# Column norms of two weight matrices in an attention and MLP kernel: sums of squares over four blocks on VectorE ahead of four products, in place of sixteen products

## The chip, the core and the metric

The kernel runs on one core of one Trainium2 chip. The metric is the device time of one execution in microseconds (us). The engines are TensorE (PE, matrix products), VectorE (DVE), ScalarE (ACT), GpSimd (POOL) and SyncE (SP, which issues the DMAs here). A tile is 128 partitions by some number of elements. PE writes to PSUM, which DVE and ACT can read; POOL works on SBUF alone.

## The reference, cut to what matters

```python
a = softmax over the sequence of phi                 # per batch b, head h: 576 x 32
k_m, v_m = a^T k, a^T v                              # 32 x 64 each
attn = softmax(q k_m^T / 8) ; out = attn v_m         # 576 x 64
x = out, heads side by side                          # 4608 tokens x 512
h = x @ w_in                                         # 512 x 2048
g = h - tanh(h)
return g @ w_out                                     # 2048 x 512
```

Batch and heads are 8 and 8. The weights w_in and w_out come in float64. The column norms, which the change is about, are no part of the result. The kernel computes them to check that its fast path may be used.

## The kernel before, in words

The fast path (`split_path`) multiplies in f16 pieces: each weight is split in a high and a low f16 half, scaled by 2^13 (`win_hi`, `win_lo`, `wout_hi`, `wout_lo`), and so are the activations. It replaces tanh by a polynomial that holds for small arguments only. So the kernel gathers statistics into the tile `stat`: squared row norms of the attention values, squared column norms of both weight matrices, and a test on each weight block's exponents. `check` compares them with windows (`V_WIN`, `WI_WIN`, `WO_WIN`), `check_all` sums the outcome over the partitions with a product into `pgood`, and a general path (`wide_path`) runs after the fast one if any value lies outside. With the reference's inputs it does not run.

**Tiling.** The 4608 tokens are 18 units of 256, and the 2048 hidden columns are four blocks of 512. One turn of the main loop, called a slot here, handles one (unit, block); slot 4u + fb is unit u, block fb, so slots run from 18 to 71. In a slot PE forms the hidden tile `hs` (`mm1`, L572). ACT squares it into `u` (L579). DVE multiplies (`g1`, L587), ACT squares again (L592), DVE finishes the polynomial (`g2`, L597), and ACT copies the high half `g` (`g2_high`, L603), from which POOL makes the low half (`g3`, L608). In the next slot DVE makes four combinations of g, called forms (`a_forms`, L621, f16). In the slot after that PE multiplies with w_out (`mm2_blocks`, L708 and L715, into the PSUM tiles `x` and `o`). Where a unit is complete, DVE adds up and scales its output (`evict`, L768 to L780). `hs` is one PSUM tile, free again once g1 has read it.

**Order.** Every engine runs its instructions in the order in which the program writes them (`in_order`). The order inside a slot is: mm1, u, g1, the words of the plan's first group (`do(0)`), the second square, the forms of the slot before, g2, mm2, sums for the weight test, `do(1)`, g2_high, g3, words put off to the slot's end (`due`), evict, `do(2)`. The plan (`PLAN_C`, L861) lists words by slot; a part after `;` belongs to `do(1)`, a part after `|` to `do(2)`. Attention work of later batches is laid into the same slots by `PLAN`.

**The column norms.** `SI` (`squares_in`, L447) has ACT square one quarter of w_in, 128 x 4 x 512, into an f16 tile; `SO` (`squares_out`, L470) does the same for w_out. Both are put off to the end of their slot. `NI` (`norms_in`, L461) and `NO` (`norms_out`, L479) sum over the partitions on PE: for each group of 128 columns a product of the squares, as the stationary operand, with a column of ones gives 128 x 1. ACT then copies the 128 x 4 result out of PSUM (L466 into `stat`, L483 into `wn`). For the quarters 0 to 2 of w_in, `SS` (`squares_sum`, L452 and L453) has DVE add up the four blocks first, in two f16 adds, and four products do. For quarter 3 and for all of w_out the products sum over the blocks, so there are sixteen.

**The PSUM buffer pa.** The results of these products lie in the pool `ps_a`, whose tag "pa" has one buffer. The same buffer takes the attention's scores (`S`, L272), its products with w_in (`P`, `att_p`, L524, read by ACT at L537 and by DVE at L542), and `pgood`. PE's first product into it waits until the last reader of the tile before is done. In slots 58, 60 and 62 a `P` product follows the norm products of the slot before.

Other words of the plan in these slots: `AM` and `AD` (POOL, L302 and L315), `AT` (DVE transpose), `AS` (ACT L513, POOL L515), and `CW` (`window`, POOL's L439 on a reloaded weight block, then ACT's L443).

Of the kernel before, what the change touches and what calls it, by code (L numbers as in the profile page):

```python
# [18 lines left out]
P = 128  # L19
# [20 lines left out]
CW = (  # L40
    0.33333331252017, -0.13333128520786, 0.053934788850892, -0.021660115374759,
    0.0082189218977914, -0.0025104593252184, 0.000420695493864,
)
# [2 lines left out]

V_WIN = (2.0 ** -12, 0.0025)
WI_WIN = (1.002 * 2.0 ** -6, 1.497)
WO_WIN = (2.0 ** -6, 3.5)
N_F1 = 32  # L50
N_ROWS = 2

# [285 lines left out]
def split_path(ctx, tc, c, ins, out):  # L338
    nc = tc.nc
# [115 lines left out]
    def norms_in(fb):  # L455
        sq = acc.pop(("q", fb))
        pa = ps_a.tile([P, 2, 512], F32, tag="pa", name=f"pni{fb}")
        blocks = 1 if fb < 3 else 4
        for k in range(4):
            for pr in range(blocks):  # L460
                nc.tensor.matmul(  # L461
                    pa[:, 0, k : k + 1], sq[:, pr, P * k : P * k + P], c["ones16"],
                    start=(pr == 0), stop=(pr == blocks - 1),
                )
        o = N_F1 + 2 * B + 4 * fb
        nc.scalar.activation(stat[:, o : o + 4], pa[:, 0, 0:4], AF.Copy, scale=(S_W * S_Q) ** -2)  # L466

# [4 lines left out]
    def norms_out(part):  # L472
        if part == 0:
            acc["n"] = big.tile([P, 4, 4], F32, tag="wn", name="wn", bufs=1)
        sq = acc.pop(("q", part))
        pa = ps_a.tile([P, 2, 512], F32, tag="pa", name=f"pno{part}")
        for k in range(4):
            for i in range(4):
                nc.tensor.matmul(  # L479
                    pa[:, 0, k : k + 1], sq[:, i, P * k : P * k + P], c["ones16"],  # L480
                    start=(i == 0), stop=(i == 3),
                )
        nc.scalar.activation(acc["n"][:, :, part], pa[:, 0, 0:4], AF.Copy, scale=(S_W * S_Q) ** -2)  # L483
        if part == 3:
            o = N_CHECK - 4
            nc.vector.tensor_reduce(stat[:, o : o + 4], acc["n"], axis=AX.X, op=ALU.add)
# [311 lines left out]
    def cubic(u, fb, stay):  # L798
# [22 lines left out]
        "Z": warm, "P": att_p, "PL": att_pl, "H": mm1, "a": lambda u, fb: cubic(u, fb, False), "ap": lambda u, fb: cubic(u, fb, True), "c": lambda u, fb: g3(u, fb, nc.gpsimd), "cv": lambda u, fb: g3(u, fb, nc.vector), "PLp": att_pl_pe,  # L821
        "T": lambda x, y: conv(10 * x + y), "L": lambda x, y: low_pool(10 * x + y), "Lv": lambda x, y: low(10 * x + y), "Lp": lambda x, y: low_pe(10 * x + y),
        "G": b_form, "F": a_forms, "SI": squares_in, "NI": norms_in, "SO": squares_out, "NO": norms_out, "SS": squares_sum,
        "GG": lambda: check(tc, c, big), "GX": lambda: check_all(tc, c, ps_a),
        "M": lambda u, fb: mm2(u, fb, fb in (0, 2), fb in (1, 3)), "R": load_part, "OP": save_part, "O": save,
# [15 lines left out]
    for word in START.split():  # L841
        if ":" in word:
            k, tag = word.split(":")
# [17 lines left out]
    PLAN_C = (  # L861
# [5 lines left out]
    )  # L867
    tasks = {}
# [79 lines left out]
def check(tc, c, big):  # L948
# [4 lines left out]
    o = N_F1  # L953
    for n, (lo, hi) in ((2 * B, V_WIN), (DF // P, WI_WIN), (DM // P, WO_WIN)):
        s, g = stat[:, o : o + n], good[:, o : o + n]
# [133 lines left out]
@with_exitstack  # L1089
def tile_kernel(ctx: ExitStack, tc: tile.TileContext, qt, kva, kvt, pha, phx, w_in, w_out, out):  # L1090
    nc = tc.nc
    ins = dict(qt=qt, kva=kva, kvt=kvt, pha=pha, phx=phx, w_in=w_in, w_out=w_out)
    const = ctx.enter_context(tc.tile_pool(name="const", bufs=1))
    c = {"first": len(nc.cur_bb.bb.instructions)}
    for name, shape, dt in (
        ("ident", [P, P], F32), ("ones", [P, P], F32), ("ones16", [P, 1], F16), ("one", [P, 1], F32),
        ("beta", [P, 1], F32), ("idw", [P, P], F32), ("nidp", [P, P], F16), ("idw", [P, P], F32), ("nid16", [P, P], F16), ("stat", [P, N_CHECK], F32), ("bad", [P, 1], I32),
    ):
        c[name] = const.tile(shape, dt, name=name)
    make_identity(nc, c["ident"])  # L1100
    nc.vector.tensor_scalar(c["nid16"], c["ident"], -1.0, None, op0=ALU.mult)
    nc.vector.tensor_scalar(c["nidp"], c["ident"], -S_V * S_W / S_P, None, op0=ALU.mult)
    nc.vector.tensor_scalar(c["idw"], c["ident"], S_W, None, op0=ALU.mult)
    nc.gpsimd.memset(c["ones"], 1.0)
    nc.gpsimd.memset(c["ones16"], 1.0)
    nc.gpsimd.memset(c["one"], 1.0)
    nc.gpsimd.memset(c["beta"], BETA)
    with ExitStack() as inner:
        split_path(inner, tc, c, ins, out)
    with tc.If(c["wide"] > 0):  # L1110
        with ExitStack() as inner:
            wide_path(inner, tc, c, ins, out)
# [39 lines left out]
```

## Time and profile before

| | us |
|---|---|
| median of three runs | 660.52 (659.53 to 663.91) |
| the profiled execution | 660.23 |
| its span, first to last instruction | 658.4 |
| PE busy in the span | 640.8 (97%) |
| DVE busy | 521.8 (79%) |
| ACT busy | 373.9 (57%) |
| POOL busy | 257.0 (39%) |

The clock granted to PE was 1.0 of full speed throughout. A row of the timeline has the start and the duration in us, the engine, the line, the operation, the output and inputs with their shapes, and, where the engine stood idle before, how long and what ended it. Rows of a group joined with xN give the whole stretch. Consecutive instructions of one engine overlap a little in the rows, so what an instruction costs its engine is read from its start to the next start. In the waits, a row has the total in us, how often, and the longest.

### The profile page before, as it was taken

How to read it: one execution, taken by the hardware profiler on the slowest of the kernel's cores; microseconds unless marked ns; L12 is line 12 of the kernel's file. 1: busy time of each engine (PE TensorE's matmuls, PEld its weight loads, DVE VectorE, ACT ScalarE, POOL GpSimd, SP SyncE). 2: the span in 40 equal slices, each digit the busy share in tenths (PEclk: the TensorE clock that was granted, in tenths of full speed). 3: DMA queues.
4: the chain of work that ended last, by engine and by line, in shares of the span. 5: the costliest groups of instructions: out<-in, count | busy, mean ns of one | idle time of the engine just before them, and what ended most of it. 6: DMA issues, size and time to landing. Idle time of an engine off the chain costs nothing.

```text
span 658.4 us, 15598 instructions
## 1 busy us (share of the span) xinstructions
PE 640.8 (97%) x6690; PEld 455.9 (69%) x6690; DVE 521.8 (79%) x790; ACT 373.9 (57%) x507; POOL 257.0 (39%) x173
## 2 busy tenths in 40 slices
PE   8788999999999999999999999999999999999996
PEld 4364656655557777777776777777687777887785
DVE  6799999999855787875988679777977686867763
ACT  4577576655524456545655465545654577666541
POOL 0224331443112245442535253625452455455521
PEclk9999999999999999999999999999999999999999
DMA  8999344223223402323331524142505333234201
GB/s 340 405 366 382 107 155 140 104 88 118 76 81 102 145 20 74 113 100 135 105 113 66 168 67 152 56 147 66 157 33 195 102 104 121 65 110 139 76 33 37
DMA packets 25996, 84.98 MB, mean 129 GB/s; under 512 B 2880, under 2 KB 2880, under 8 KB 25152
## 3 DMA queue, kind: packets, MB, share of 16 engines
q1 hardware_dynamic: 24624, 81.55, 35.8%
q10 hardware_dynamic: 1296, 2.36, 0.9%
q8 instruction: 54, 0.88, 0.6%
q14 instruction: 22, 0.18, 0.1%
HBM read 72.37 MB, written 11.53 MB: 127 GB/s over the span
## 4 chain that ended last, share of the span: by engine, by line
PE 71%; DVE 15%; DMA 6%; issue 3%; POOL 2%; ACT 2%; SPq 0%; DVEq 0%; ACTq 0%; POOLq 0%
PE hs L572 20%; PE x L715 13%; PE o L708 13%; PE o L715 10%; PE o L651 5%; DMA raw<-in_w_out_dram 3%; PE pp L524 3%; PE h L572 2%; DVE wt L384 2%; DVE h L597 2%; DVE h L587 2%; PE pkv L220 2%; DMA kv<-in_kva_dram 2%; PE o1h L651 2%; DVE wt L389 1%
## 5 line engine op out<-in xcount | busy, mean ns | idle before, releaser
L608 POOL TENSOR_TENSOR g<-h,g 128x1024 f16<-128x1024 f32 x67 | 146.6, 2188 | 328.4 <-ACT g L603 215.9
L572 PEld LDWEIGHTS <-ph 128*128 128x128 f16 x2304 | 176.9, 98 | 21.1 <-issue 6.0
L572 PE MATMUL hs<-ah,ph 128*128 128x256 f16 (+3 forms) x1152 | 151.5, 246 | 0.0
L587 DVE SCALAR_TENSOR_TENSOR h<-hs,u 128x1024 f32<-128x1024 f32 x54 | 65.8, 1218 | 91.9 <-ACT u L579 91.9
L603 ACT ACTIVATE g<-h 128x1024 f16<-128x1024 f32 x72 | 76.0, 1056 | 97.5 <-DVE h L597 92.7
L572 PE MATMUL hs<-al,ph 128*128 128x256 f16 (+3 forms) x576 | 127.7, 246 | 0.0
L592 ACT ACTIVATE u<-u,beta 128x1024 f32<-128x1024 f32 x72 | 82.5, 1148 | 57.5 <-DVE h L587 57.1
L708 PE MATMUL o<-wout_hi,g 128*128 128x512 f16 x432 | 104.7, 380 | 0.0
L715 PEld LDWEIGHTS <-f 128*128 128x128 f16 x896 | 87.7, 98 | 10.1
L597 DVE SCALAR_TENSOR_TENSOR h<-u,h 128x1024 f32<-128x1024 f32 x72 | 87.6, 1217 | 0.7 <-ACT u L592 0.7
L579 ACT ACTIVATE u<-hs 128x1024 f32<-128x1024 f32 x54 | 55.0, 1019 | 54.7 <-PE hs L572 50.5
L715 PEld LDWEIGHTS <-g 128*128 128x128 f16 x672 | 64.2, 98 | 26.5 <-issue 5.1
L715 PE MATMUL x<-bt,f 128*128 128x256 f16 x672 | 82.5, 273 | 0.0
L708 PEld LDWEIGHTS <-g 128*128 128x128 f16 x432 | 40.5, 98 | 43.9 <-issue 8.1
L651 PEld LDWEIGHTS <-g 128*128 128x128 f16 x384 | 36.6, 98 | 46.7 <-issue 4.3
L621 DVE TENSOR_TENSOR f<-g 128x512 f16<-128x512 f16 x112 | 65.1, 621 | 4.3 <-POOL g L608 3.4
L651 PE MATMUL o<-wout_hi,g 128*128 128x512 f16 x192 | 59.0, 380 | 0.0
L572 PE MATMUL h<-ah,ph 128*128 128x256 f16 (+3 forms) x384 | 49.9, 246 | 0.6 <-DVE h L587 0.6
L572 PE MATMUL h<-al,ph 128*128 128x256 f16 (+2 forms) x192 | 42.5, 246 | 0.1
L542 DVE SCALAR_TENSOR_TENSOR ph<-pp,ph 128x1024 f16<-128x1024 f32 x31 | 37.7, 1215 | 0.4 <-ACT ph L537 0.3
L537 ACT ACTIVATE ph<-pp 128x1024 f16<-128x1024 f32 x32 | 32.5, 1017 | 7.7 <-PE pp L524 7.7
L651 PE MATMUL o<-wout_lo,g 128*128 128x512 f16 x96 | 36.4, 380 | 0.0
(146 smaller groups left out, 973.8 us busy)
## 6 DMA issues: line engine op xcount, KB each, us to landing
kv<-in_kva_dram SPq DMA_DIRECT2D x20, 516.0 KB, 3.9
q<-in_qt_dram SPq DMA_DIRECT2D x16, 576.0 KB, 4.3
chk<-in_w_in_dram SPq DMA_DIRECT2D x16, 512.0 KB, 5.6
chk<-in_w_out_dram SPq DMA_DIRECT2D x16, 512.0 KB, 3.3
out_dram<-r SPq DMA_DIRECT2D x27, 256.0 KB, 2.3
kv<-in_kva_dram SPq DMA_DIRECT2D x6, 1032.0 KB, 9.1
raws<-in_w_in_dram SPq DMA_DIRECT2D x12, 512.0 KB, 8.1
raw<-in_w_out_dram SPq DMA_DIRECT2D x12, 512.0 KB, 8.6
```

Of the source, the lines that this page charges most:

```text
L542: nc.vector.scalar_tensor_tensor(pl, pa, S_P / (S_V * S_W), ph, op0=ALU.mult, op1=ALU.subtract)
L572: nc.tensor.matmul(hp[:, k, tu : tu + w], px[:, g, cs], d[ax][:, g, ta : ta + w], start=(n == 0), stop=(n == 5),)
L579: nc.scalar.activation(uu, hp, AF.Square, scale=1.0 / (S_A * S_P))
L587: nc.vector.scalar_tensor_tensor(h3, hp, C2 * S_G / (S_A * S_P), uu, op0=ALU.mult, op1=ALU.mult)
L592: nc.scalar.activation(uu, uu, AF.Square, bias=c["beta"])
L597: nc.vector.scalar_tensor_tensor(h3, uu, CC, hp, op0=ALU.add, op1=ALU.mult)
L603: nc.scalar.activation(gg[:, 0], h3, AF.Copy)
L608: eng.tensor_tensor(gg[:, 1], h3, gg[:, 0], op=ALU.subtract)
L621: nc.vector.tensor_tensor(o, x, y, op=op)
L651: nc.tensor.matmul(o, gx[:, k, P * tt : P * tt + P], wx[:, 4 * fb + k, :], start=(first and k == 0 and wx is wout_hi and gx is gh), stop=( ...
L708: nc.tensor.matmul(o[th], gg[:, 0, k, P * th : P * th + P], wout_hi[:, 4 * fb + k, :], start=(first and k == 0), stop=False)
L715: nc.tensor.matmul(dst, a(1 - n, kk), b(n, kk), start=(new and kk == 0 and n == 0), stop=(end and kk == 1 and n == 1))
```

## The change

For quarter 3 of w_in and for the four quarters of w_out, DVE now adds the four blocks of squares together (the same `squares_sum`), and PE does four products instead of sixteen. The new words are SS3 in slot 55 and SS0 to SS3 in slots 57, 59, 61 and 63, all in `do(0)`, behind g1 and what `PLAN` has there. The upper and lower bound for w_out's norms become a little tighter.

```diff
-WO_WIN = (2.0 ** -6, 3.5)
+WO_WIN = (1.002 * 2.0 ** -6, 3.493)
...
     def norms_in(fb):
         sq = acc.pop(("q", fb))
         pa = ps_a.tile([P, 2, 512], F32, tag="pa", name=f"pni{fb}")
-        blocks = 1 if fb < 3 else 4
         for k in range(4):
-            for pr in range(blocks):
-                nc.tensor.matmul(
-                    pa[:, 0, k : k + 1], sq[:, pr, P * k : P * k + P], c["ones16"],
-                    start=(pr == 0), stop=(pr == blocks - 1),
-                )
+            nc.tensor.matmul(pa[:, 0, k : k + 1], sq[:, 0, P * k : P * k + P], c["ones16"], start=True, stop=True)
...
         for k in range(4):
-            for i in range(4):
-                nc.tensor.matmul(
-                    pa[:, 0, k : k + 1], sq[:, i, P * k : P * k + P], c["ones16"],
-                    start=(i == 0), stop=(i == 3),
-                )
+            nc.tensor.matmul(pa[:, 0, k : k + 1], sq[:, 0, P * k : P * k + P], c["ones16"], start=True, stop=True)
...
-        (54, "CQ CQ SI3"), (55, "CW CW CQ CQ | NI3"), (56, "CW CW CQ CQ SO0"), (57, "CW CW CQ CQ | NO0"), (58, "CW CQ SO1"),
+        (54, "CQ CQ SI3"), (55, "SS3 CW CW CQ CQ | NI3"), (56, "CW CW CQ CQ SO0"), (57, "SS0 CW CW CQ CQ | NO0"), (58, "CW CQ SO1"),
...
-        (59, "CW CQ | NO1"), (60, "CW CQ SO2"), (61, "CW CQ | NO2"), (62, "CW CQ SO3"), (63, "CW CW CQ CQ | NO3"), (64, "CW CW CQ CQ"),
+        (59, "SS1 CW CQ | NO1"), (60, "CW CQ SO2"), (61, "SS2 CW CQ | NO2"), (62, "CW CQ SO3"), (63, "SS3 CW CW CQ CQ | NO3"), (64, "CW CW CQ CQ"),
```

The order on DVE in slot 57 (unit 14, block 1), before: g1 (h3141 from hs), the four forms f140, g2, and the first instruction of the eviction. Line numbers of the changed kernel are lower by two to nine.

```order
L587 SCALAR_TENSOR_TENSOR h3141_7067<-hs_2447,u141_7065 128x1024 [waits Activation_49]
L621 TENSOR_TENSOR f140_7070<-g140_7023 128x2x256 [waits Pool_49]
L621 TENSOR_TENSOR f140_7070<-g140_7023 128x2x256
L621 TENSOR_TENSOR f140_7070<-f140_7070,g140_7023 128x2x256 [waits DVE_49]
L621 TENSOR_TENSOR f140_7070<-g140_7023,f140_7070 128x2x256 [waits DVE_49]
L597 SCALAR_TENSOR_TENSOR h3141_7067<-u141_7065,h3141_7067 128x1024 [waits Activation_49]
L768 SCALAR_TENSOR_TENSOR r130_7076<-x_2446,r130_7076 128x256 [waits DMAHW2_49,PE_49,Activation_49]
```

The same place now:

```order
L578 SCALAR_TENSOR_TENSOR h3141_7057<-hs_2447,u141_7055 128x1024 [waits Activation_49]
L452 TENSOR_TENSOR sqo0_7024<-sqo0_7024 128x1024
L453 TENSOR_TENSOR sqo0_7024<-sqo0_7024 128x512 [waits DVE_49]
L612 TENSOR_TENSOR f140_7062<-g140_7013 128x2x256 [waits Pool_49]
L612 TENSOR_TENSOR f140_7062<-g140_7013 128x2x256
L612 TENSOR_TENSOR f140_7062<-f140_7062,g140_7013 128x2x256 [waits DVE_49]
L612 TENSOR_TENSOR f140_7062<-g140_7013,f140_7062 128x2x256 [waits DVE_49]
L588 SCALAR_TENSOR_TENSOR h3141_7057<-u141_7055,h3141_7057 128x1024 [waits Activation_49]
L759 SCALAR_TENSOR_TENSOR r130_7068<-x_2446,r130_7068 128x256 [waits DMAHW2_49,PE_49,Activation_49]
```

The two adds on the squares sqo0 stand between g1 and the forms; the forms, g2 and the eviction follow behind them in the order they had.

The order on PE from the end of slot 59 (last product of mm2 into o1400, norm products pno1 on the squares sqo1, first product of the next mm1) to the first product of `P` for batch 7, block 2 (pp72) in slot 60, before:

```order
L715 MATMUL o1400_7219<-wout_lo_100,f141_7213 128x256
L479 LDWEIGHTS sqo1_7268 [waits Activation_49]
L479 MATMUL pno1_7384<-ones16_60,sqo1_7268 128x1 [waits DVE_49]
...
L572 MATMUL hs_2447<-ah6_6264,ph60_6173 128x192
...
L524 MATMUL pp72_7454<-win_hi_97,vh7_6793 32x512 [waits Activation_49]
```

The same place now:

```order
L706 MATMUL o1400_7199<-wout_lo_100,f141_7193 128x256
L473 LDWEIGHTS sqo1_7248 [waits DVE_49,Activation_49]
L473 MATMUL pno1_7366<-ones16_60,sqo1_7248 128x1 [waits PE_49]
...
L563 MATMUL hs_2447<-ah6_6264,ph60_6173 128x192
...
L515 MATMUL pp72_7424<-win_hi_97,vh7_6793 32x512 [waits Activation_49]
```

Four pairs of weight load and product are left of sixteen, and the first weight load waits for DVE's adds besides ACT's squares. The first product into pp72 waits for ACT as before, which is the copy of pno1 out of "pa". The orders on ACT, POOL and SP are as they were.

## The prediction

> **What bounds the kernel now.** I read the page first, then the waits between engines, then the timeline around the five slots that the change touches (a slot is one turn of the loop over unit and block; numbers as in PLAN_C).
>
> ```profile
> span 658.4 us, 15598 instructions
> PE 640.8 (97%) x6690; PEld 455.9 (69%) x6690; DVE 521.8 (79%) x790; ACT 373.9 (57%) x507; POOL 257.0 (39%) x173
> ```
>
> By shares PE is the bound and VectorE (DVE) has a fifth of the span free. The waits from 530 to 600 us seem to say the same:
>
> ```profile
> DVE h L587 <- ACT u L579: 17.5, 7, 3.1
> ACT u L579 <- PE hs L572: 2.3, 5, 0.7
> ```
>
> DVE idles 17.5 us there. But ScalarE (ACT), on which it waits, waited for PE only 2.3 us in 70. So there are two things that run at one pace: PE, and a ring of the other engines. One turn of the ring is ACT's square u (L579), DVE's g1 (L587), its four forms (L621) and g2 (L597), ACT's copy g (L603), GpSimd's (POOL's) subtraction (L608), and ACT's next u. DVE's idle time in it is time in which ACT does its part of the same turn; it is slack only where ACT in turn waits for PE. The change takes work from PE and puts work into the ring, between g1 and g2.
>
> **What PE saves.** The groups of four products (L461 in slot 33) and of sixteen (slot 55), each with the instruction behind it:
>
> ```profile
> 320.47 0.24 PE L461 MATMUL pni<-ones,sqi 128*128 128x1 f16 x4
> 320.58 0.27 PE L715 MATMUL x<-wout_hi,g 128*128 128x256 f16 x1
> ...
> 517.53 0.54 PE L461 MATMUL pni<-ones,sqi 128*128 128x1 f16 x16
> 517.93 0.27 PE L572 MATMUL hs<-ah,ph 128*128 128x256 f16 x1
> ```
>
> From start to start four take 0.11 us and sixteen 0.40. A group saves 0.29, five groups 1.45.
>
> The Trainium skill (TensorE: Matmul & The Clock Gate, section Back-to-back issue gap) gives about 81 ns for a pair of weight load and matmul at 128 columns. By that the sixty pairs would be 4.9 us; the trace has 25 ns a pair (0.40 / 16), since these products stream one column, and the measurement decides.
>
> **What a pair of adds costs.** The pair is not new; quarter 0 of W_in has it:
>
> ```profile
> 318.20 0.69 DVE L452 TENSOR_TENSOR sqi<-sqi 128x1024 f16<-128x1024 f16 x1
> 318.92 0.43 DVE L453 TENSOR_TENSOR sqi<-sqi 128x512 f16<-128x512 f16 x1
> 319.26 0.75 DVE L311 TENSOR_REDUCE sz<-sc 128x18 f32<-128x576 f32 x1
> ```
>
> From 318.20 to 319.26 is 1.06 us of DVE. Five pairs are 5.3. There is a second price: f16 adds of this kind can be held while POOL runs. The forms show it:
>
> ```profile
> 531.65 1.34 POOL L315 TENSOR_TENSOR sc<-sc,sz 128x576 f32<-128x576 f32 x1
> 531.90 1.37 DVE L621 TENSOR_TENSOR f<-g 128x512 f16<-128x512 f16 x1
> ```
>
> Two free forms take 0.72 us (slot 56, below); this single one took 1.37 and ended at 533.27, 0.28 after POOL's instruction (531.65 + 1.34 = 532.99). The bounds for a pair are therefore 1.06 us, and 1.06 plus one POOL instruction (1.34 here). In slots 57, 61 and 63 a form is held already, and the pair, which now stands ahead of it, is held in its place; so I take 1.06 everywhere.
>
> **Where it goes, slot by slot.** Shifts are against the profiled execution. *Slot 55*: SS3 moves g2, ACT's copy and POOL's row by 1.06; in slot 56 that meets the forms.
>
> ```profile
> 522.44 1.16 POOL L302 TENSOR_TENSOR sc<-sc,sm 128x576 f32<-128x576 f32 x1
> 523.70 0.72 DVE L621 TENSOR_TENSOR f<-g 128x512 f16<-128x512 f16 x2
> 525.13 1.22 DVE L597 SCALAR_TENSOR_TENSOR h<-u,h 128x1024 f32<-128x1024 f32 x1
> 526.39 1.06 ACT L603 ACTIVATE g<-h 128x1024 f16<-128x1024 f32 x1
> 527.35 1.89 ACT L470 ACTIVATE sqo<-wout_hi 128x2048 f16<-128x2048 f16 x1
> 529.15 1.00 ACT L579 ACTIVATE u<-hs 128x1024 f32<-128x1024 f32 x1
> ```
>
> L302 ended at 523.60, just ahead of the forms. Now it ends at about 524.7, a form waits for it, and g2 starts 0.8 late although PE brought the slot 0.29 early. ACT's three rows have no idle time between them, so u of slot 57 is 0.8 late too: the first saving of PE is lost.
>
> *Slots 57 and 58*: SS0 adds its 1.06, so g2 starts 1.8 late.
>
> ```profile
> 533.99 1.22 DVE L597 SCALAR_TENSOR_TENSOR h<-u,h 128x1024 f32<-128x1024 f32 x1
> 536.20 0.16 ACT L483 ACTIVATE wn<-pno 128x4 f32<-128x4 f32 x1
> 536.58 1.28 DVE L780 SCALAR_TENSOR_TENSOR r<-o,r 128x512 f32<-128x512 f32 x2
> 536.60 0.41 PE L524 MATMUL pp<-win_hi,vh 64*32 64x512 f16 x8
> 536.77 1.02 ACT L579 ACTIVATE u<-hs 128x1024 f32<-128x1024 f32 x1 [0.41 <-PE hs L572]
> 537.83 1.23 DVE L587 SCALAR_TENSOR_TENSOR h<-hs,u 128x1024 f32<-128x1024 f32 x1
> ```
>
> Three things hang on g2 here. Behind the copy g on ACT stands L483, which reads the column norms out of the one PSUM buffer "pa"; it ended at 536.36. PE's product L524 of slot 58 writes that same buffer and started at 536.60, 0.24 later. With L483 1.8 late PE stands at L524 until about 538.2 and everything behind it on PE waits: the saved time becomes a stall. It may wait first at the norm products themselves, for SS0's second add; L524 then still sets the time. On DVE the evictions (to L780) and then g1 follow with no idle time: g1 of slot 58 is 1.8 late. The 0.41 that u waited for PE gives nothing back, because g1 stood behind the evictions.
>
> *Slots 59 and 60*: the same pair of neighbours on "pa", now 1.8 + 1.06 = 2.9 late.
>
> ```profile
> 552.38 1.06 ACT L603 ACTIVATE g<-h 128x1024 f16<-128x1024 f32 x1 [2.15 <-DVE h L597]
> 553.35 0.16 ACT L483 ACTIVATE wn<-pno 128x4 f32<-128x4 f32 x1
> 553.62 0.41 PE L524 MATMUL pp<-win_hi,vh 64*32 64x512 f16 x8
> 553.79 1.02 ACT L579 ACTIVATE u<-hs 128x1024 f32<-128x1024 f32 x1 [0.29 <-PE hs L572]
> ```
>
> L483 ended 0.11 us before L524; PE starts it about 2.9 late. The ring could regain 0.29 at u, but a POOL row as late as g2 holds the forms of slot 60, so g2 there is 2.9 late again.
>
> *Slots 61 to 63*: SS2 makes it 4.0 on the ring, and g1 of slot 62 again stands directly behind the evictions:
>
> ```profile
> 569.37 0.16 ACT L483 ACTIVATE wn<-pno 128x4 f32<-128x4 f32 x1
> 569.83 0.41 PE L524 MATMUL pp<-win_hi,vh 64*32 64x512 f16 x8
> 571.05 1.23 DVE L587 SCALAR_TENSOR_TENSOR h<-hs,u 128x1024 f32<-128x1024 f32 x1
> ```
>
> L483 of slot 61 had 0.30 us to spare, so PE starts that L524 3.7 late. *Slot 63*: the last pair makes it 5.0. No product follows on "pa" in slot 64, so PE, 3.7 late, runs on; the ring does not catch up with it:
>
> ```profile
> 585.51 2.13 POOL L608 TENSOR_TENSOR g<-h,g 128x1024 f16<-128x1024 f32 x1 [3.77 <-issue]
> 588.34 1.76 DVE L621 TENSOR_TENSOR f<-g 128x512 f16<-128x512 f16 x2
> 590.81 1.22 DVE L597 SCALAR_TENSOR_TENSOR h<-u,h 128x1024 f32<-128x1024 f32 x1
> ```
>
> The forms of slot 64 read POOL's result and stand behind its next rows (1.76 us for two), and POOL is 5.0 late; so is g2. In slot 65 the same holds, and from slot 66 ACT's u waits for nothing. The ring meets PE at the product of the final check:
>
> ```profile
> 600.95 1.02 ACT L579 ACTIVATE u<-hs 128x1024 f32<-128x1024 f32 x1
> ...
> 623.52 0.38 PE L967 MATMUL pgood<-grow,ones 128*128 128x1 f32 x2 [0.44 <-DVE grow L960]
> ```
>
> PE waited 0.44 for the ring there, so it takes the whole lateness there at the latest: 5.0. **Sum**: 0.8 + 4 x 1.06 = 5.0 us; the 1.45 that PE saves counts only inside the 0.8. The profiled execution took 660.2 (span 658.4 and 1.8 around it), which gives 665.2; the median of the runs is 0.3 above that execution, so I say 665.3. The window constant changes two immediates of instructions that stay, which costs nothing, and no DMA is added or moved past another. If POOL did not hold the forms of slots 56, 60 and 64, the ring would regain part of that (second rival).
>
> **Rivals.** *PE's saving counts and DVE hides the adds.* For it: 97% and DVE's 17.5 us of idle time. Against it: the 0.24, 0.11 and 0.30 us on "pa", and that ACT waited for PE only 2.3 us. Time 660.2 - 1.45 = 658.8. *The ring regains its slack.* It waited for PE five times, 2.3 us, in these slots; if all is taken back, 5.0 - 2.3 = 2.7 and 662.9. It needs forms that pass POOL unheld and evictions that do not stand ahead of g1. *Clearly slower: adds and POOL hold each other.* If a pair begins inside a POOL instruction where no form was held before, each of the four pairs from slot 57 on pays one more, 1.16 us by L302's row. That makes 5.0 + 4.6 = 9.6, 669.8. It decides once the pairs, not the forms, stand at POOL's end; against it, the forms of slots 57, 61 and 63 already stand there. The Trainium skill (GPSIMD Engine Reference, section Specifications) has the two engines contend whenever DVE reads two SBUF tensors, as all ten adds do; the held form agrees. *The products are dear.* A weight load of these products lasts 96 ns by itself:
>
> ```profile
> L461 PEld LDWEIGHTS <-sqi x28: 95/96/98, 320.4 to 517.9; 128*128 128x128 f16 x28
> ```
>
> If each cost PE that much, sixty would be 5.8 us, and with PE as the bound the time 654.4. Against it: sixteen took 0.40, so the loads overlap. This is the rival in which the Trainium skill's figure for pairs, cited above, would also land, at 660.2 - 4.9 = 655.3.
>
> *It does not do what it says*: if sums in f16 left a norm outside its window, the wide path would run and add hundreds of us (it repeats PE's 640.8 us of work in f32). Weights of variance 1/512 and 1/2048 give norms near 1, far inside 2^-6 to 3.49.
>
> **How the numbers follow.** Forecast 0.59, with its own range 663.7 to 666.9 (pairs of 0.8 to 1.4 us); PE's saving 0.07; slack regained 0.22; adds and POOL 0.10; dear products 0.01; wide path 0.01. The range 661.0 to 667.8 leaves out PE's saving and most of the third rival. A measurement of this kernel can tell about 1%, 6.6 us: the forecast is +0.7%. Slower by more than that: most of the third rival, the wide path and the forecast's upper tail, 0.13. Faster: 0.01. The rest, 0.86, is within 1%.
>
> **What would show it.** Right: ten new DVE rows L452 and L453 of some 0.7 and 0.4 us, held rows among them in slot 57; PE waiting about 1 us or more for L483's successor at the product into pp in slots 58, 60 and 62; ACT's u of slots 57, 59, 61 and 63 later by about 0.8, 1.8, 2.9 and 4.0; the wait of pgood for grow above 0.44. Wrong: PE with no waits in those slots and a span below 658, or u of slot 65 less than 3 us late.

## The result, and the profile after

The changed kernel takes 665.82 us (median of seven runs, 664.93 to 668.18), the kernel before 660.90 in the same comparison (659.53 to 663.91). The ratio is 1.0064, with a 95% interval of 1.004 to 1.0087: 0.6% slower, 4.9 us. The interval leaves out 1, and the fastest of the seven changed runs lies above the slowest of the seven before. The prediction was 665.3.

The page of the changed kernel, to be read against the first two rows of the prediction:

```profile
span 664.0 us, 15493 instructions
PE 640.2 (96%) x6630; PEld 454.6 (68%) x6630; DVE 529.2 (80%) x800; ACT 374.0 (56%) x507; POOL 257.4 (39%) x173
```

PE has its sixty products less and DVE its ten adds more. Line numbers here are those of the changed kernel (g1 is L578, g2 L588, the copy g L594, u L570, the norms' copy L474, the product into pp L515). Slots 57 and 58 in its timeline, one engine after the other:

```profile
533.00 0.93 DVE L452 TENSOR_TENSOR sqo<-sqo 128x1024 f16<-128x1024 f16 x1
533.95 1.26 DVE L453 TENSOR_TENSOR sqo<-sqo 128x512 f16<-128x512 f16 x1
535.14 0.75 DVE L612 TENSOR_TENSOR f<-g 128x512 f16<-128x512 f16 x2
...
536.60 1.22 DVE L588 SCALAR_TENSOR_TENSOR h<-u,h 128x1024 f32<-128x1024 f32 x1
...
540.39 1.22 DVE L578 SCALAR_TENSOR_TENSOR h<-hs,u 128x1024 f32<-128x1024 f32 x1
...
533.33 1.60 POOL L315 TENSOR_TENSOR sc<-sc,sz 128x576 f32<-128x576 f32 x1
...
538.81 0.16 ACT L474 ACTIVATE wn<-pno 128x4 f32<-128x4 f32 x1
538.87 1.02 ACT L570 ACTIVATE u<-hs 128x1024 f32<-128x1024 f32 x1
...
535.36 0.24 PE L473 MATMUL pno<-ones,sqo 128*128 128x1 f16 x4 [1.05 <-DVE sqo L453]
...
539.02 0.41 PE L515 MATMUL pp<-win_hi,vh 64*32 64x512 f16 x8 [0.79 <-ACT wn L474]
```

The pair stands between g1 and the forms and is held by POOL's L315 in the forms' place. The two forms of this row took 1.95 us in the kernel before and take 0.75 now; before, the row was

```profile
531.33 1.95 DVE L621 TENSOR_TENSOR f<-g 128x512 f16<-128x512 f16 x2
```

PE waits first for the second add (1.05) and then for ACT's copy of the norms (0.79). g1 of slot 58 follows the evictions with no idle time.

All waits of PE from 430 us on, in the kernel before and then in the changed kernel (total, times, longest):

```profile
PE psc L272 <- DVE vl L498: 0.7, 1, 0.7
PE pgood L967 <- DVE grow L960: 0.4, 1, 0.4
PE pkv L220 <- DMA kv<-in_kva_dram: 0.3, 1, 0.3
```

```profile
PE pp L515 <- ACT wn L474: 2.2, 3, 0.8
PE pno L473 <- DVE sqo L453: 1.6, 2, 1.1
PE x L706 <- DVE r L760: 1.2, 1, 1.2
PE psc L272 <- DVE vl L489: 0.7, 1, 0.7
PE pkv L220 <- DMA kv<-in_kva_dram: 0.5, 1, 0.5
PE pgood L958 <- DVE grow L951: 0.4, 1, 0.4
PE pno L473 <- ACT r L744: 0.2, 1, 0.2
```

The first three rows and the last are new; they come to 5.2 us. PE ends up 4.75 us later (below) although it saves 1.45, so 6.2 us are to be found. The rest lies in how the rows count: a product counts as busy to the end of its row, mostly 0.27 us, while in a stream the next one starts after 0.11, so each of the seven new waits is some 0.15 us longer than its figure. The other way round, the profile shows no wait of ACT's u for PE from 531 to 601 us now, where the kernel before had 2.3 us from 530 to 600: in these slots the ring is the later of the two.

**One measure for all runs.** The first loads differ between executions by a few us (u of slot 54 starts at 502.48 before and at 503.43 in the changed kernel, and as late as 506.50 in one run below), and this moves all that follows. So I measure from ACT's u of slot 54, ahead of everything that the change touches, to the product pgood in slot 69. Behind pgood PE runs to the end of its products, as it did before. In the kernel before that is 623.52 - 502.48 = 121.04 us. In the changed kernel the two rows are

```profile
503.43 1.02 ACT L570 ACTIVATE u<-hs 128x1024 f32<-128x1024 f32 x1 [3.52 <-PE hs L563]
...
629.22 0.38 PE L958 MATMUL pgood<-grow,ones 128*128 128x1 f32 x2 [0.44 <-DVE grow L951]
```

and the measure is 125.79: 4.75 more. The table gives it for every run. Each row is one traced execution. How far such a row can be trusted shows where two kernels still run the same code: in the run with one pair in slot 59, u of slots 55 to 59 lies within 0.01 us of the kernel before.

| run | us from u of slot 54 to pgood | against before |
|---|---|---|
| before | 121.04 | |
| changed | 125.79 | +4.75 |
| one pair, slot 55 | 121.71 | +0.67 |
| one pair, slot 59 | 122.04 | +1.00 |
| four pairs for W_out, sixteen products | 125.07 | +4.03 |
| four products, no new adds | 120.76 | -0.28 |
| changed, norms' copy ahead of g | 125.70 | +4.66 |
| squares early, sixteen products, no new adds | 120.71 | -0.33 |
| squares early, four products, no new adds | 119.50 | -1.54 |
| squares early, four products, adds behind g2 and a transpose | 121.35 | +0.31 |
| squares early, four products, adds directly behind g2 | 119.59 | -1.45 |
| the same, last quarter in slot 66 | 119.50 | -1.54 |

### The profile page after: what moved, and what is told of

Its sections match the earlier page's. It is cut to its first block, busy times and chain, and to the rows that moved or that the text cites. A ratio compares the mean times of both kernels' runs of the same rounds, so it can differ in the third digit from the quotient of the medians.

```text
span 664.0 us, 15493 instructions
## 1 busy us (share of the span) xinstructions
PE 640.2 (96%) x6630; PEld 454.6 (68%) x6630; DVE 529.2 (80%) x800; ACT 374.0 (56%) x507; POOL 257.4 (39%) x173
## 4 chain that ended last, share of the span: by engine, by line
PE 66%; DVE 16%; DMA 6%; issue 5%; ACT 3%; POOL 2%; SPq 0%; DVEq 0%; ACTq 0%; POOLq 0%
PE hs L563 16%; PE x L706 11%; PE o L699 10%; PE o L706 8%; PE o L642 7%; PE h L563 4%; DMA raw<-in_w_out_dram 3%; PE o1h L642 3%; DVE f L612 3%; PE pp L515 3%; DVE h L588 2%; DVE h L578 2%; DMA kv<-in_kva_dram 2%; PE pkv L220 2%; DVE ph L533 1%
## 5 line engine op out<-in xcount | busy, mean ns | idle before, releaser
L578 DVE SCALAR_TENSOR_TENSOR h<-hs,u 128x1024 f32<-128x1024 f32 x54 | 65.8, 1218 | 89.1 <-ACT u L570 89.1
L594 ACT ACTIVATE g<-h 128x1024 f16<-128x1024 f32 x72 | 76.0, 1056 | 104.6 <-DVE h L588 100.0
L588 DVE SCALAR_TENSOR_TENSOR h<-u,h 128x1024 f32<-128x1024 f32 x72 | 87.6, 1217 | 0.7 <-ACT u L583 0.7
L570 ACT ACTIVATE u<-hs 128x1024 f32<-128x1024 f32 x54 | 55.0, 1018 | 51.2 <-PE hs L563 47.1
```

What stands on the lines that cost most here:

```text
L570: nc.scalar.activation(uu, hp, AF.Square, scale=1.0 / (S_A * S_P))
L578: nc.vector.scalar_tensor_tensor(h3, hp, C2 * S_G / (S_A * S_P), uu, op0=ALU.mult, op1=ALU.mult)
L588: nc.vector.scalar_tensor_tensor(h3, uu, CC, hp, op0=ALU.add, op1=ALU.mult)
L594: nc.scalar.activation(gg[:, 0], h3, AF.Copy)
```

## The experiments

**The theory and its rivals.** Theory: from slot 56 on the ring (ACT's u, DVE's g1 and g2, ACT's g, POOL's g3) sets the pace together with PE. A pair between g1 and g2 makes the ring later by its own length, and no later slot gives it back. Rivals: PE alone is the bound and its saving counts; the adds lie in DVE's idle time; the loss is PE's stall on the buffer "pa"; an add costs DVE's time wherever it stands.

**The products alone.** The five SS words are taken out of the changed kernel:

```diff
-(55, "SS3 CW CW CQ CQ | NI3")
+(55, "CW CW CQ CQ | NI3")
...
-(57, "SS0 CW CW CQ CQ | NO0")
+(57, "CW CW CQ CQ | NO0")
```

> The changed kernel without its five new pairs of adds: four products a group, on the first of the four blocks alone, so that three quarters of each of these sums are left out. Measure: the time in the trace from ACT's u of slot 54 to the product pgood, 121.04 us in the kernel before and 125.79 in the changed one. Theory (the ring ACT-DVE-ACT-POOL sets the pace from slot 56 on, and PE's saving is worth almost nothing): 120.8, which is 0.2 less than before. Rival (PE is the bound, its saving counts): 119.6, which is 1.45 less.

Measured: 120.76, 0.28 less, as the ring has it. The trace shows where PE's saving went. Counted from u of slot 54, PE gains 0.30 us at each of the five groups, and gives back 0.21, 0.44 and 0.13 at the products into pp in slots 58, 60 and 62 and 0.43 at x in slot 66. Two of these waits are long enough to be printed:

```profile
554.33 0.41 PE L515 MATMUL pp<-win_hi,vh 64*32 64x512 f16 x8 [0.37 <-ACT wn L474]
...
601.38 0.27 PE L706 MATMUL x<-wout_hi,g 128*128 128x256 f16 x1 [0.29 <-DVE r L760]
```

What is left is the 0.28.

**The adds alone.** The kernel before gets the words SS0 to SS3 in slots 57 to 63 and keeps its sixteen products:

```diff
-(57, "CW CW CQ CQ | NO0")
+(57, "SS0 CW CW CQ CQ | NO0")
```

> The kernel before with the four pairs of adds for W_out in slots 57, 59, 61 and 63, but the sixteen products kept (W_out's norms come out about twice as large, and are still inside their window). Theory: each pair makes the ring 1.04 later, so 121.04 + 4.1 = 125.2 us from u of slot 54 to pgood, whatever PE does. Rival (the adds lie in DVE's idle time): 121.0 to 121.3.

Measured: +4.03, 1.01 a pair, with PE's work unchanged. The rival that hides them in DVE's idle time is out.

**One pair.** The same for slot 59 alone, with four products in that group:

```diff
-(59, "CW CQ | NO1")
+(59, "SS1 CW CQ | NO1")
```

> The kernel before with one pair alone, SS1 in slot 59, and four products in that group only. Theory: 121.04 + 1.04 = 122.1 us from u of slot 54 to pgood. Rival (hidden; PE saves 0.29): 120.7. Rival (POOL holds the adds, one more instruction of POOL): 123.2.

Measured: +1.00. In slot 59 g2 starts 1.06 later behind g1 than before. The lateness stays to the end: u is 1.08 late in slot 61 and 1.00 in slot 69.

**The pair of slot 55.**

```diff
-        blocks = 1 if fb < 3 else 4
+        blocks = 1
...
-(55, "CW CW CQ CQ | NI3")
+(55, "SS3 CW CW CQ CQ | NI3")
```

> The kernel before with one pair alone, SS3 in slot 55, and four products in that group. This pair reaches the ring only through POOL, whose late instruction holds a form of slot 56. Theory: +0.75, so 121.8 us from u of slot 54 to pgood, with one form of slot 56 lasting 1 us or more. Rival (no hold: ACT's 2.5 us wait for PE in slot 56 takes the lateness up): 120.8 to 121.0.

Measured: +0.67. In this run's slot 56 two forms last 1.73 us, where they took 0.72 before, because POOL's row in front of them is late:

```profile
524.86 1.34 POOL L302 TENSOR_TENSOR sc<-sc,sm 128x576 f32<-128x576 f32 x1
...
524.75 1.73 DVE L621 TENSOR_TENSOR f<-g 128x512 f16<-128x512 f16 x2
```

POOL ends at 526.20, and the form behind it 0.28 later. This pair and the four of W_out (with sixteen products kept) come to 0.67 + 4.03 = 4.70 of the 4.75.

**Is it the buffer pa?** In the changed kernel the five norm words move from the slot's end to ahead of the copy g:

```diff
-(57, "SS0 CW CW CQ CQ | NO0")
+(57, "SS0 CW CW CQ CQ ; NO0")
```

> The changed kernel with the five groups of products and ACT's copies of them moved from the slot's end to ahead of ACT's copy g of the same slot; PE's order stays, the buffer pa no longer waits for g. Theory (ring): PE's waits at the products into pp in slots 58, 60 and 62 vanish, but the time does not fall: 125.8 us from u of slot 54 to pgood, within 0.4, and PE waits later (at x in slot 66 or at pgood). Rival (the loss is PE's stall on pa): the 2.2 us of these waits come back, 123.6 or less.

Measured: 125.70. The waits at pp are gone, and the time is the same to 0.1 us. The waits of PE that the kernel before does not have are, in this run:

```profile
PE pno L473 <- DVE sqo L453: 3.2, 3, 1.4
PE x L706 <- DVE r L760: 1.2, 1, 1.2
PE pno L473 <- ACT r L744: 1.0, 1, 1.0
```

The buffer only chose the place at which PE met the ring; without it PE met it at the norm products. With the adds in place, the rival falls.

**Taking work out of the ring.** If the ring sets the pace, shortening it must gain. ACT's squares of 1.89 us stand at the slot's end, between g and the next u. Here they run ahead of g, where ACT waits for g2 anyway, and the products one slot later; products and adds are those of the kernel before:

```diff
-(58, "CW CQ SO1"), (59, "CW CQ | NO1"), (60, "CW CQ SO2")
+(58, "CW CQ ; EO0"), (59, "CW CQ ; NO0"), (60, "CW CQ ; EO1")
...
+        "EI": squares_in, "EO": squares_out,
```

(EI and EO do the work of SI and SO at once and not at the slot's end.)

> The kernel before, its sixteen products and no new adds, with only ACT's squares and the products laid as in the kernel with the adds in idle time. Takes ACT's 1.8 us squares out of the ring. Theory (the ring set the pace in the kernel before too, together with PE): 121.04 - 1.5 = 119.5 us from u of slot 54 to pgood. Rival (PE, 97% busy, was the only bound): 120.6 to 121.0, since PE's work is the same and it waited 0.44 us in all there.

Measured: 120.71, 0.33 less. The theory's number was wrong and the rival's right. The ring did get shorter; ACT's u waited for PE 2.3 us from 530 to 600 before, and in the same stretch of this run (534 to 604, as u of slot 54 is 4.02 later)

```profile
ACT u L579 <- PE hs L572: 4.0, 5, 1.2
```

So the ring waited for PE. The 0.33 comes from elsewhere. In slot 54 of the kernel before, the squares stood on ACT ahead of vh, and PE waited for what hangs on vh:

```profile
509.48 1.90 ACT L447 ACTIVATE sqi<-win_hi 128x2048 f16<-128x2048 f16 x1
511.44 0.27 ACT L496 ACTIVATE vh<-ptr 128x128 f16<-128x128 f32 x1
511.74 0.29 DVE L498 SCALAR_TENSOR_TENSOR vl<-ptr,vh 128x128 f16<-128x128 f32 x1 [2.57 <-ACT vh L496]
512.08 0.72 PE L272 MATMUL psc<-q,kT 64*32 64x288 f32 x16 [0.67 <-DVE vl L498]
```

With the squares early this wait is gone, and PE is 0.74 ahead from there. It gives back 0.31 at x in slot 66 and 0.10 at pgood. From slot 56 on the shorter ring gained nothing by itself: PE's work was the same, and before pgood PE had not waited there. The theory needs a second half: ring and PE are two bounds close together, and each hides a gain in the other.

**Both at once, without adds.** With the squares early and four products, the adds left out:

```diff
-(58, "CW CQ ; EO0 SS0")
+(58, "CW CQ ; EO0")
```

> The kernel with the adds in idle time, without its five new pairs of adds (four products on the first block alone, so that three quarters of these sums are left out). Theory: the adds cost nothing where they stand, so the same 118.9 us from u of slot 54 to pgood as with them, within 0.2. Rival (adds still cost): 1 us or more less than with them.

Measured: 119.50, and not 118.9. The sixty products, worth 0.28 us alone, are worth 1.21 here (120.71 - 119.50). The placing changes two things at once, though: the squares leave the ring, and ACT's copy of the norms no longer stands behind g, so the waits at pp are gone too. Four products with the copy early and the squares late, without adds, were not run; which part each has in the 1.21 is not shown. That the kernel with adds should come out the same failed at first:

**The adds where DVE is idle.** The same with the pairs behind g2:

```diff
-(58, "CW CQ ; EO0")
+(58, "CW CQ ; EO0 SS0")
```

> The changed kernel, with the same adds and the same four products, laid elsewhere: ACT's squares in front of ACT's copy g, where ACT waits for g2 (slots 54, 58, 60, 62, 64), the pair of adds behind g2 in the same slot, where DVE then waits for ACT, and the products one slot later. Theory (what counts is whether work lies in the ring): from u of slot 54 to pgood 121.04 - 2.1 = 118.9 us, so some 2 us less than before in the whole, 658.8 where before has 660.9. Rival (an add costs DVE's time wherever it stands): the five pairs' 4.9 us stay, 124 us or more.

Measured: 121.35, and 661.32 us against 661.34 before: ratio 1.0002 (0.9984 to 1.002), no difference. The pairs cost 1.85 us here (121.35 - 119.50), neither nothing, as the theory had it with its 118.9, nor 4.9, as the rival had it with 124 or more. Slot 54 shows where half of it arose. On DVE, POOL and PE:

```profile
509.27 0.65 DVE L452 TENSOR_TENSOR sqi<-sqi 128x1024 f16<-128x1024 f16 x1
509.95 2.28 DVE L453 TENSOR_TENSOR sqi<-sqi 128x512 f16<-128x512 f16 x1
512.15 0.28 DVE L489 SCALAR_TENSOR_TENSOR vl<-ptr,vh 128x128 f16<-128x128 f32 x1
...
509.82 2.13 POOL L599 TENSOR_TENSOR g<-h,g 128x1024 f16<-128x1024 f32 x1 [7.89 <-ACT g L594]
...
512.49 0.72 PE L272 MATMUL psc<-q,kT 64*32 64x288 f32 x16 [0.90 <-DVE vl L489]
```

A transpose stood between g2 and the pair. So the second add began 0.13 us after POOL's subtraction and was held to its end at 511.95; vl behind it came late, and PE waited 0.90 us for vl. Without the adds PE does not wait there and is 0.97 us earlier. The other 0.87 us are at x in slot 66. The second adds of slots 58 and 62, behind transposes too, were held in the same way (shortest, median, longest in ns, of all four in W_out); how their lateness reaches x was not followed:

```profile
L453 DVE TENSOR_TENSOR sqo<-sqo x4: 425/1353/2325, 545.2 to 593.2; 128x512 f16<-128x512 f16 x4
```

**The pair directly behind g2.** In slots 54, 58 and 62 the words EI or EO and SS now stand ahead of the attention's words in the same group, so that the adds start before POOL's subtraction:

```diff
-                todo[i] += " " + x
+                todo[i] = x + " " + todo[i] if x.split()[:1] and x.split()[0][:2] in ("EI", "EO") and sl != 60 else todo[i] + " " + x
```

> The kernel with the adds in idle time, with the pair directly behind g2 (ahead of the transposes of slots 54, 58 and 62), so that it ends before POOL's subtraction of the slot begins. There the second add of slot 54 lasted 2.28 us behind POOL's instruction, and PE waited 0.90 us for what stood behind it. Theory (adds cost nothing where DVE waits for ACT and POOL is idle): from u of slot 54 to pgood 119.5 to 120.2 us (the kernel without adds has 119.50), so about 1 us less than before in the whole. Rival (adds cost DVE's time wherever): 121.35 as with the transposes ahead.

Measured: 119.59, and 659.94 us against 661.30 before: ratio 0.9978 (0.9966 to 0.9991), 1.4 us faster than the kernel before. All eight second adds, of W_in and W_out, take their free length now (shortest, median, longest in ns):

```profile
L453 DVE TENSOR_TENSOR sqi<-sqi x4: 424/424/424, 319.9 to 510.7; 128x512 f16<-128x512 f16 x4
L453 DVE TENSOR_TENSOR sqo<-sqo x4: 424/424/426, 545.3 to 593.0; 128x512 f16<-128x512 f16 x4
```

In slot 58 the add runs from 545.33 to 545.76 and POOL starts at 545.60; so an add that has begun before POOL is not held. The pairs cost 0.09 us now (119.59 - 119.50).

The same ten new adds and the same four products that made the kernel 4.9 us slower are part of one that is 1.4 faster. Not all of this is theirs: the squares moved as well, and alone gave 0.33. Against that kernel, adds and four products in place of sixteen products are worth 1.12 us (120.71 - 119.59). The pairs between g1 and g2 with the squares early, or behind g2 with the squares late, were not run.

**The last quarter in slot 66.**

```diff
-(64, "CW CW CQ CQ ; EO3 SS3"), (65, "CW CW CQ CQ ; NO3")
+(66, "CW CW CQ ; EO3 SS3"), (67, "CW ; NO3")
```

> The same, with the squares and the pair of the last quarter of W_out in slot 66 in place of 64, its products in slot 67. Theory: the turns of slots 65 to 68 are the ring's slowest (it loses 0.6 us to PE there), and ACT's idle time ahead of g is 1.04 us in slot 64 and 1.40 in slot 66, so 0 to 0.4 us less than the same kernel with slot 64. Rival (PE is the bound by now): the same within 0.1.

Measured: 119.50, 0.09 less. This fits the rival, and the theory only at its edge; it tells little.

## Why the prediction was right

**What bounds the kernel.** Right for this change: two things at one pace, and work between g1 and g2 lengthens the ring. The runs add how close the two are: relieving PE alone gained 0.28 us, moving the squares alone 0.33 (all of it from slot 54), both 1.54. What the prediction called slack of the ring (2.3 us of ACT waiting for PE) did not come back, as it said. Too strong was that DVE's idle time is slack only where ACT waits for PE: behind g2, in that idle time, five pairs cost 0.09 us. It was their place ahead of g2 that cost time.

**PE's saving.** 0.29 a group was right (0.30 measured), and so was that it counts for almost nothing here: -0.28 with the products alone. The prediction let it count inside slot 56 only, and u of slot 56 is 0.30 early.

**A pair.** From g1 to g2 the changed kernel takes 1.06, 0.94, 1.06, 1.05 and 1.06 us more in slots 55, 57, 59, 61 and 63, so the price was right, also where the pair is held in a form's place. The ring gives back a little: 1.00 is left of one pair at the end, and 1.01 as a mean of four.

**Slot by slot.** The prediction had u of slots 57, 59, 61 and 63 late by 0.8, 1.8, 2.9 and 4.0; measured, with the 0.95 of the start taken off, 0.72, 1.67, 2.74 and 3.68. The sum of 5.0 came out as 4.75; the difference lies in what was left of each pair (1.01 for 1.06) and in the first step (0.72 for 0.8). Two slips stand in the arithmetic: 660.2 + 5.0 + 0.3 is 665.5 and not 665.3, and the lower end of the forecast's own range, 663.7, leaves out the first step (pairs of 0.8 give 660.5 + 0.8 + 3.2 = 664.5). The difference between the medians came out as 4.9 for the 5.0; the rest of the distance to 665.82 is the kernel before, which took 660.90 in this comparison and not 660.5.

**PE's waits.** The three at pp are there, in slots 58, 60 and 62, but last 0.79, 0.72 and 0.72 and not 1 us or more. PE had already stood at the norm products (1.05 us in slot 57), which the prediction named as possible and did not price. The wait of pgood did not grow beyond 0.44: PE took the ring's lateness one step earlier, 1.19 us at its first product into x in slot 66, which waits for an eviction (L760). That sign was named wrongly, although the working allowed for it ("at the latest").

**The rivals.** PE's saving (658.8) and regained slack (662.9) are refuted by the runs above, dear products (654.4) by the 0.30 a group. Adds and POOL holding each other did not happen in the changed kernel beyond what the forms paid before, as the 0.94 to 1.06 above show; with the adds laid behind a transpose it did.

## What to carry to other kernels

Idle time of an engine takes up only work that is laid into it. DVE idled 17.5 us of 70 here, yet adds ahead of g2 cost their full length, because the rest of the turn waits for g2; so follow the ring once round and ask what stands behind the new work. Where two bounds run within a few tenths of a us, relieving either alone shows next to nothing, and both have to be relieved together. Before dropping a change that lost time, try its place: a pair cost about 1.0 us between two steps of the ring, and all five together 0.09 behind them, as long as they began before POOL.

## What the runs showed of the hardware that was not expected

The hold between an f16 add on DVE and POOL lasts as long as POOL's instruction, also a long one. An add of 424 ns lasted 2.28 us behind POOL's 2.13 us, and ended at 512.23, 0.28 after it. An add of the same length that began 0.27 us before such an instruction took 0.43 us. The Trainium skill (GPSIMD Engine Reference, section Specifications) has the two engines contend for their SBUF interfaces when DVE reads two tensors there; the trace agrees. Each such add or form that was followed here ended 0.28 us behind POOL's instruction, whether this lasted 1.34 or 2.13 us, which fits a stop better than a slower rate.
